# Attention and two feed-forward networks in one kernel: decoding of weight units, the softmax sum and the order of the steps rearranged

## Chip, cores and metric

One core of one Trainium2 chip runs the whole kernel as one program. The metric is the device time of one execution in microseconds. Times inside the program are counted from the start of its span; the execution's own time is a little longer than the span.

## What is computed

```python
def reference(q, k, v, w_in, w_out, w1, w2, w3, w_out2):
    # attention: B=2, H=8, S=768, D=64
    k_sum = k.reshape(B, H, 24, 32, D).max(axis=3)
    v_sum = v.reshape(B, H, 24, 32, D).mean(axis=3)
    local = where(|i - j| < 16, scale * q @ k.T, -1e9)
    block = scale * q @ k_sum.T + log(32)
    s = concatenate([local, block]); s = s - s.max()
    a = exp(s); a = a / (a.sum() + 1e-9)
    x = a @ concatenate([v, v_sum])         # as 1536 rows of 512
    # network 1, 512 -> 2048 -> 512
    h = x @ w_in;  x = (h - tanh(h)) @ w_out
    # network 2, 512 -> 1024 -> 512
    return ((x @ w1) * (x @ w2)) @ w3 @ w_out2
```

All inputs and outputs are float32. Query and key are wide enough that exp(s) has a real spread.

## The kernel before, in words

Every large product is made with operands split into a high and a low part, so that one product is three matmuls on TensorE: high by high, low by high, high by low (helper `split_mm`, lines 238 to 240). 128x512 is the usual tile.

**Weight units.** The weights come in 512 KB units of 128x512 words of 64 bits, loaded by SP in a fixed sequence (four buffers). A unit is decoded to float32 in steps: ScalarE makes `bits` (line 145); then either VectorE makes three operations (158, 160, 162), or, for units in the table `PLAN["SIGN"]`, ScalarE makes a second activation into the upper half of `dec` (149) and VectorE two operations (152, 154). A unit's high part `wh` is copied on GpSimd (191) or, for units in `PLAN["ACT"]`, on ScalarE (193); its low part `wl` is a subtraction on GpSimd (200). Units that are started while the attention runs keep `bits` in PSUM; only these can take the form with two operations.

**Stage 1, attention, 0 to about 117 us.** The work is 24 groups g, each of 4 query tiles of one pair of heads. Group g goes through S(g) (scores, TensorE), M0 to M3 (mask and maximum, VectorE), E0 to E3 (exponentials with their sum z, ScalarE), R(g) (z + 1e-9 as a sum over two columns, line 450, and its reciprocal, 451, both VectorE), PP(g) (product, GpSimd, 455), T(g) (transposes, TensorE), PB(g) (copy `pt`, ScalarE, 467), V(g) (product with the values, TensorE), XH(g) (high part, ScalarE, 488) and XL(g) (low part, VectorE, 243). V has one PSUM buffer, so V(g+1) waits for XL(g). At every third group V also makes the block means of the next pair of heads, which ScalarE copies (`vr`, 399) and SP writes into the values with three small DMAs (404). The key maxima K0 to K2 are made on VectorE and copied by GpSimd (379).

Beside this TensorE makes w34 = w3 @ w_out2 in 32 *parts* of six matmuls; these need weight units, and they are the work that fills TensorE. After four parts the sums are copied by ScalarE (337) or added by VectorE (335).

The order is written by hand as tables. Step g runs through one of three lists in `PLAN["L"]` (steps 0 and 1, steps 2 to 16, from 17); an entry such as `("T", 2)` issues T(g-2), `("S", -1)` issues S(g+1). `W0` and `W1` issue the step's parts, whose number is `PLAN["N34"][g]`; `D`, `U`, `H`, `L` and `ST` move the weight units on. Each engine runs its instructions in the order in which the lists issue them.

**Stage 2, network 1, 117 to about 375 us.** 48 steps of 24 matmuls on TensorE; the other engines make h - tanh(h) and decode the remaining units. Entry min(n, 8) of `PLAN["MIDDLE"]` is the order of step n.

**Stage 3, network 2, to the end.** The first third of the rows goes through plain products (`product_a`, `half`, `product_b`, `final`, with `w34_split` making the two parts of w34), the others through seven products instead of eight for each two by two block (`group`, `w_sums`).

Of the kernel before, what the change touches and what calls it, by code (L numbers as in the profile page):

```python
# [7 lines left out]
F32 = mybir.dt.float32  # L8
# [5 lines left out]
AF = mybir.ActivationFunctionType  # L14
ALU = mybir.AluOpType
# [6 lines left out]
P = 128  # L22
# [4 lines left out]
QT = 64  # L27
# [25 lines left out]
PLAN = {"cuts": [2, 17], "N34": [0, 0, 0, 0, 0, 2, 0, 2, 2, 0, 2, 1, 2, 1, 2, 0, 1, 2, 3, 1, 2, 1, 1, 3, 1, 2, 3],  # L53
        "MORE": (15, 18, 22), "MOREU": (20, 24, 32),
        "SIGN": (1, 3, 5, 7, 9, 11, 13, 14, 15, 17, 19, 20, 21, 22, 23, 24, 26, 27, 28, 29, 32, 35, 39, 41, 43, 45, 47, 49, 51, 53, 55, 57, 59, 61, 63, 65, 67, 69, 71, 73, 75, 77, 79), "ACT": (0, 4, 7, 8, 16, 19, 22, 25, 27, 28, 29, 31, 33, 35)}
PLAN["L"] = [
# [14 lines left out]
]  # L71
PLAN["MIDDLE"] = [
# [17 lines left out]
def fused_kernel(tc, qT, kT, vW, w_in, w_out, w1, w2, w3, wo2, out):  # L90
# [156 lines left out]
    with tc.tile_pool(name="base", bufs=1) as base, \  # L247
# [9 lines left out]
        nc.gpsimd.memset(numax, -UMAX)  # L257
        band = base.tile([P, WK], F32, name="band")
# [7 lines left out]

        mean = base.tile([P, 6 + BLK], F32, name="mean")
        nc.gpsimd.memset(mean, 0.0)

        def rows(col, a, b):  # L270

            nc.gpsimd.memset(col, 1.0 / BLK)
            for base_, step in ((-a, 1), (b - 1, -1)):
                nc.gpsimd.affine_select(out=col, in_=col, pattern=[[0, 1]], compare_op=ALU.is_ge, fill=0.0,
                                        base=base_, channel_multiplier=step)

        rest = base.tile([P, 1], F32, name="mean_rest")
        rows(mean[:, 6:7], WIN, WIN + BLK)
        rows(mean[:, 7:8], WIN + BLK, QT)
        rows(rest, CW, CW + WIN)  # L280
        nc.gpsimd.tensor_tensor(out=mean[:, 7:8], in0=mean[:, 7:8], in1=rest, op=ALU.add)
        masks = []
        for z in range(3):
            mk = base.tile([P, NC], F32, name=f"mask{z}")
            nc.gpsimd.memset(mk[:, BC], LOG_BLK)
            nc.gpsimd.tensor_copy(out=mk[:, :QT], in_=band[:, :QT])
            nc.gpsimd.tensor_copy(out=mk[:, CW:], in_=band[:, QT:])
            if z == 0:
                nc.gpsimd.memset(mk[:, :WIN], NEG)
            if z == 2:  # L290
                nc.gpsimd.memset(mk[:, NC - WIN:], NEG)
            masks.append(mk)
# [46 lines left out]
        with tc.tile_pool(name="p1", bufs=1) as p1, \  # L339
# [41 lines left out]
            sums = [p1.tile([P, TU, 2], F32, tag=f"z{i}", name=f"z_{i}") for i in range(3)]  # L381
            for i in sums:
                nc.vector.memset(i[:, :, 1], 1e-9)
# [47 lines left out]
            def mx(g, i):  # L431
                t = g % NU * TU + i
                mk = masks[0 if t == 0 else 2 if t == NQ - 1 else 1]
                if g not in nm:
                    nm[g] = p1.tile([P, TU], F32, tag="nm", bufs=3, name=f"nm_{g}")
                    pr[g] = p1.tile([P, TU, NC], F32, tag="pr", bufs=3, name=f"pr_{g}")
                    z[g] = sums[g % 3]
                nc.vector.tensor_tensor_reduce(  # L438
                    out=pr[g][:, i, :], in0=st[g][i % len(st[g])][:, i, :], in1=mk[:, :], scale=-0.125, scalar=3.0e38,
                    op0=ALU.add, op1=ALU.min, accum_out=nm[g][:, i:i + 1])  # L440

            def ex(g, i):
# [67 lines left out]
            scores(0)  # L510
            n34 = 0
# [68 lines left out]
            acts = dict(S=do_S, R=do_R, PP=do_PP, T=do_T, PB=do_PB, V=do_V, XH=do_XH, XL=do_XL)  # L580
# [395 lines left out]
        for m in range(1, NM):  # L976
# [7 lines left out]
            a = product_a(m, 0)  # L984
            wt.unit(1)
# [39 lines left out]
        for m in range(0, NM, 2):  # L1025
# [84 lines left out]
```

## Time and profile before

| what | us |
|---|---|
| runs | 574.33, 574.31, 571.29 (median 574.31) |
| the profiled execution, its own time | 572.8 |
| its span | 571.1 |
| TensorE busy | 556.0 |
| VectorE busy | 456.1 |
| ScalarE busy | 335.1 |
| GpSimd busy | 292.0 |

The trace gives for each engine the instructions with start, duration, and the idle time ahead of them with what released it. Matmuls overlap, so the time between two starts is less than a matmul's listed duration. On ScalarE and VectorE, too, the next instruction starts a little before the listed end of the one ahead.

### The profile page before, as it was taken

What the parts mean: (1) busy time and instruction counts of PE and PEld (TensorE: products, weight loads), DVE (VectorE), ACT (ScalarE), POOL (GpSimd) and SP (SyncE); (2) the same over time, 40 slices, a digit from 0 to 9 for tenths busy, and PEclk for the clock granted to TensorE, in tenths of its full rate; (3) what the DMA queues carried; (4) which work ended last, traced back from release to release, by engine and by line L of the source; (5) the groups of instructions that cost most, each with busy time, mean ns of one, the idle gap of its engine ahead of it and who ended that gap; (6) DMA issues with size and microseconds to landing.
All of it is one profiled execution on the core that took longest, in us unless ns stands there. A gap on an engine that the chain in (4) does not pass through costs nothing.

```text
span 571.1 us, 9225 instructions
## 1 busy us (share of the span) xinstructions
PE 556.0 (97%) x3224; PEld 450.0 (79%) x3224; DVE 456.1 (80%) x880; ACT 335.1 (59%) x739; POOL 292.0 (51%) x257
## 2 busy tenths in 40 slices
PE   6699999999999999999999999999999999999997
PEld 5477777778888888888888888888788877888885
DVE  4878899998899999889999769999378677868510
ACT  4799888876978876577766667845233321213110
POOL 4766775834464655535645315466536653617220
PEclk9899999999999999999999999999999999999999
DMA  8998777441232332122223003222000100000021
GB/s 329 352 312 287 279 242 231 143 146 38 74 111 76 110 100 84 37 84 87 88 82 102 1 2 110 75 73 75 0 1 1 74 1 1 1 0 1 1 92 55
DMA packets 18526, 56.56 MB, mean 99 GB/s; under 512 B 1968, under 2 KB 4656, under 8 KB 18480
## 3 DMA queue, kind: packets, MB, share of 16 engines
q1 hardware_dynamic: 18336, 55.84, 29.6%
q8 instruction: 25, 0.41, 0.3%
q14 instruction: 21, 0.17, 0.1%
q10 hardware_dynamic: 144, 0.13, 0.1%
HBM read 51.64 MB, written 3.15 MB: 96 GB/s over the span
## 4 chain that ended last, share of the span: by engine, by line
PE 81%; DVE 9%; issue 3%; ACT 3%; DMA 2%; SPq 1%; POOL 0%; DVEq 0%; ACTq 0%
PE ph L238 7%; PE ph L239 7%; PE ph L240 7%; PE x L238 7%; PE x L239 7%; PE x L240 7%; PE p_w L238 5%; PE p_w L240 5%; PE p_w L239 4%; PE o L240 4%; PE o L239 4%; PE o L238 4%; PE w34a L238 2%; DMA raw<-wo 2%; PE w34a L239 2%
## 5 line engine op out<-in xcount | busy, mean ns | idle before, releaser
L243 POOL TENSOR_TENSOR gl<-g,gh 128x512 fp32r<-128x512 f32 x48 | 65.0, 1354 | 127.1 <-ACT gh L729 69.4
L200 POOL TENSOR_TENSOR wl<-dec,wh 128x512 fp32r<-128x512 f32 x72 | 111.7, 1553 | 18.1 <-ACT wh L193 14.5
L238 PE MATMUL x<-gh,wh 128*128 128x512 f32 x192 | 74.9, 390 | 0.0
L238 PE MATMUL ph<-xh,wh 128*128 128x512 f32 x192 | 74.8, 390 | 0.0
L239 PE MATMUL x<-gl,wh 128*128 128x512 f32 x192 | 74.7, 389 | 0.0
L240 PE MATMUL ph<-xh,wl 128*128 128x512 f32 x192 | 74.7, 389 | 0.0
L239 PE MATMUL ph<-xl,wh 128*128 128x512 f32 x192 | 74.7, 389 | 0.0
L240 PE MATMUL x<-gh,wl 128*128 128x512 f32 x192 | 74.7, 389 | 0.0
L707 ACT ACTIVATE u<-ph 128x512 f32<-128x512 f32 x48 | 28.8, 600 | 52.0 <-PE ph L240 52.0
L162 DVE SCALAR_TENSOR_TENSOR dec<-raw,dec 128x512 uint32<-128x512 uint32 x48 | 48.6, 1013 | 1.5
L718 DVE TENSOR_TENSOR g<-ph,u 128x512 f32<-128x512 f32 x48 | 33.0, 687 | 17.6 <-ACT th L708 16.1
L720 DVE SCALAR_TENSOR_TENSOR g<-sq,g 128x512 f32<-128x512 f32 x48 | 45.3, 943 | 0.6 <-ACT sq L713 0.5
L243 POOL TENSOR_TENSOR s_w<-s_w,s_w 128x512 fp32r<-128x512 f32 x16 | 23.1, 1460 | 42.9 <-ACT s_w L937 23.2
L193 ACT CAST wh<-dec 128x512 fp32r<-128x512 f32 x54 | 33.7, 624 | 15.9 <-DVE dec L162 15.7
L238 PEld LDWEIGHTS x<-gh,wh 128*128 128x128 f32 x192 | 36.1, 188 | 7.9 <-DVE x2a L755 0.4
L443 ACT ACTIVATE pr<-pr,nm 128x120 f32<-128x120 f32 x96 | 37.9, 401 | 7.2 <-DVE nm L438 7.2
L240 PEld LDWEIGHTS x<-gh,wl 128*128 128x128 f32 x192 | 36.0, 188 | 7.5
L238 PEld LDWEIGHTS ph<-xh,wh 128*128 128x128 f32 x192 | 36.0, 188 | 7.5
L239 PEld LDWEIGHTS ph<-xl,wh 128*128 128x128 f32 x192 | 36.1, 188 | 7.4
L240 PEld LDWEIGHTS ph<-xh,wl 128*128 128x128 f32 x192 | 36.0, 188 | 7.5
L239 PEld LDWEIGHTS x<-gl,wh 128*128 128x128 f32 x192 | 36.0, 188 | 7.5 <-POOL gl L243 0.2
L724 DVE COPY_PREDICATED g<-mk,ph 128x512 f32<-128x512 uint32 x48 | 36.0, 749 | 3.9
(164 smaller groups left out, 1426.8 us busy)
## 6 DMA issues: line engine op xcount, KB each, us to landing
raw<-w SPq DMA_DIRECT2D x32, 512.0 KB
raw<-w_in SPq DMA_DIRECT2D x16, 512.0 KB
raw<-w_out SPq DMA_DIRECT2D x16, 512.0 KB
vg<-vW SPq DMA_DIRECT2D x8, 768.0 KB
raw<-wo SPq DMA_DIRECT2D x8, 512.0 KB
kt<-kT SPq DMA_DIRECT2D x7, 544.0 KB
qt<-qT SPq DMA_DIRECT2D x7, 384.0 KB
out<-u_out SPq DMA_DIRECT2D x6, 256.0 KB
```

What stands on the lines that cost most here:

```text
L162: lambda tu=tu, su=su, lo=lo: stt(out=tu, in0=lo, scalar=29, in1=su, op0=ALU.logical_shift_right, op1=ALU.bitwise_or)])
L193: nc.scalar.copy(out=h, in_=self.t[n])
L200: nc.gpsimd.tensor_tensor(out=l, in0=self.t[self.n_low], in1=h[:, :].bitcast(F32), op=ALU.subtract)
L238: mm(out=acc, lhsT=lh, rhs=rh, start=start, stop=False)
L239: mm(out=acc, lhsT=lh, rhs=rl, start=False, stop=False)
L240: mm(out=acc, lhsT=ll, rhs=rh, start=False, stop=stop)
L243: eng.tensor_tensor(out=out, in0=x, in1=high.bitcast(F32), op=ALU.subtract)
L443: nc.scalar.activation(out=pr[g][:, i, :], in_=pr[g][:, i, :], func=AF.Exp, scale=-1.0, bias=nm[g][:, i:i + 1], accum_out=z[g][:, i, :1])
L707: nc.scalar.activation(out=u, in_=ph, func=AF.Square)
L718: nc.vector.tensor_tensor(out=gn, in0=ph, in1=u, op=ALU.mult)
L720: nc.vector.scalar_tensor_tensor(out=gn, in0=sq, scalar=GAM, in1=gn, op0=ALU.add, op1=ALU.mult)
L724: nc.vector.copy_predicated(out=gn, mask=mask[:, :].bitcast(U32), data=ph)
```

## The change

- `PLAN["SIGN"]` grows: of the units that are started during the attention, 21 instead of 16 are decoded with two VectorE operations, and ScalarE has the second activation for the five more.
- The column of 1e-9 and the reduction over two columns are gone. A new step Z(g) adds 1e-9 to z on ScalarE with a bias tile `eps`; R(g) is the reciprocal alone.
- The lists `PLAN["L"]` have another order and the new entry Z; `PLAN["N34"]` places the parts otherwise (the first two in step 4 instead of 5; none in steps 5, 8 and 20); `MORE`, `MOREU` and the first eight entries of `MIDDLE` differ.
- The masks and `mean` are made on GpSimd behind the first key maxima, not ahead of them.
- In stage 3 `w34_split(m)` stands ahead of the unit's step and the calls of `high` and `low` ahead of it are gone; in the loop over `group` the second `next(g)` comes ahead of `w_sums`.

```diff
-PLAN = {"cuts": [2, 17], "N34": [0, 0, 0, 0, 0, 2, 0, 2, 2, 0, 2, 1, 2, 1, 2, 0, 1, 2, 3, 1, 2, 1, 1, 3, 1, 2, 3],
+PLAN = {"cuts": [2, 17], "N34": [0, 0, 0, 0, 2, 0, 1, 2, 0, 1, 2, 1, 1, 2, 1, 1, 1, 2, 3, 1, 0, 3, 1, 3, 2, 1, 3],
...
+        eps = base.tile([P, 1], F32, name="eps")
+        nc.gpsimd.memset(eps, 1e-9)
...
-            sums = [p1.tile([P, TU, 2], F32, tag=f"z{i}", name=f"z_{i}") for i in range(3)]
-            for i in sums:
-                nc.vector.memset(i[:, :, 1], 1e-9)
...
-                    z[g] = sums[g % 3]
+                    z[g] = p1.tile([P, TU], F32, tag="z", bufs=3, name=f"z_{g}")
...
+            def softmax_z(g):
+                nc.scalar.activation(out=z[g], in_=z[g], func=AF.Identity, bias=eps[:])
 
             def softmax_r(g):
                 rs[g] = r = p1.tile([P, TU], F32, tag="r", bufs=2, name=f"r_{g}")
-                nc.vector.tensor_reduce(out=r, in_=z[g], axis=AX.X, op=ALU.add)
-                nc.vector.reciprocal(out=r, in_=r)
+                nc.vector.reciprocal(out=r, in_=z[g])
...
             a = product_a(m, 0)
+            w34_split(m)
             wt.unit(1)
...
-            if m > 2:
-                wt.high()
-                wt.low()
-            w34_split(m)
             final(*prev)
...
             next(g)
+            next(g)
             sums = w_sums("w2", m)
             next(sums)
-            next(g)
             lhs = next(sums)
```

The order on GpSimd at the start of the program, before (`kt` is the key tile that the copy completes, `pr` the probabilities):

```order
L281 TENSOR_TENSOR mean<-mean,mean_rest 128x1
L285 MEMSET mask_102 128x24
L286 COPY mask_102<-band 128x64
L287 COPY mask_102<-band 128x32
...
L291 MEMSET mask_111 128x16
L379 COPY kt_156<-kb_176 128x12x24
L455 TENSOR_TENSOR pr_189<-pr_189,r_248 128x480
```

And now, behind the making of `band`:

```order
L267 AFFINE_SELECT band<-band 64x96
L355 COPY kt_125<-kb_145 128x12x24
L489 MEMSET mask_157 128x24
L490 COPY mask_157<-band 128x64
L491 COPY mask_157<-band 128x32
...
L511 TENSOR_TENSOR mean<-mean,mean_rest 128x1
L430 TENSOR_TENSOR pr_185<-pr_185,r_243 128x480
```

The copy into `kt` moved ahead of the three masks and of `mean`.

On TensorE, from V(0) on, before (`av` is V's bank, `t` T's, `s` S's, `w34a` the sums of w34):

```order
L477 MATMUL av_366<-pt_299,vg_164 64x64 x8
L394 MATMUL av_366<-vg_201,mean 32x128 x12
L462 MATMUL t_405<-ident,pr_245 120x128 x4
L428 MATMUL s_3_425<-kt_166,qt_168 64x120 x2
L428 MATMUL s_4_426<-kt_166,qt_168 64x120 x2
...
L477 MATMUL av_445<-pt_344,vg_164 64x64 x8
L238 MATMUL w34a_0_460<-wh_294,wh_321 128x512
L239 MATMUL w34a_0_460<-wl_295,wh_321 128x512
L240 MATMUL w34a_0_460<-wh_294,wl_322 128x512
```

And now:

```order
L452 MATMUL av_364<-pt_309,vg_133 64x64 x8
L367 MATMUL av_364<-vg_198,mean 32x128 x12
L239 MATMUL w34a_0_398<-wh_301,wh_316 128x512
L240 MATMUL w34a_0_398<-wl_302,wh_316 128x512
L241 MATMUL w34a_0_398<-wh_301,wl_317 128x512
...
L437 MATMUL t_417<-ident,pr_246 120x128 x4
L401 MATMUL s_3_422<-kt_135,qt_137 64x120 x2
...
L452 MATMUL av_455<-pt_356,vg_133 64x64 x8
```

Part 0 moved ahead of T(2), S(5) and V(1); part 1 stands between S(5) and V(1).

On ScalarE at the second weight unit, before:

```order
L145 ACTIVATE bits_215<-raw_162 128x512
L443 ACTIVATE pr_207,z_143<-pr_207,nm_206 128x120 x4
L399 COPY vr_258<-pvs 96x128
L145 ACTIVATE bits_267<-raw_170 128x512
L149 ACTIVATE dec_266<-raw_170 128x512
L443 ACTIVATE pr_245,z_144<-pr_245,nm_244 128x120 x2
L193 CAST wh_294<-dec_214 128x512
```

And now:

```order
L146 ACTIVATE bits_209<-raw_131 128x512
L416 ACTIVATE pr_185,z_186<-pr_185,nm_184 128x120 x2
L422 ACTIVATE z_186<-z_186,eps 128x4
L416 ACTIVATE pr_203,z_204<-pr_203,nm_202 128x120 x2
L146 ACTIVATE bits_257<-raw_139 128x512
L150 ACTIVATE dec_256<-raw_139 128x512
L372 COPY vr_265<-pvs 96x128
L416 ACTIVATE pr_203,z_204<-pr_203,nm_202 128x120
```

The second unit's two activations moved ahead of two of group 1's exponentials and of the copy `vr`, and the new activation of z stands between the exponentials.

## Rows read from the trace of the kernel before

**Rows 1.** The page, its first part: busy time of each engine.

```profile
PE 556.0 (97%) x3224; PEld 450.0 (79%) x3224; DVE 456.1 (80%) x880; ACT 335.1 (59%) x739; POOL 292.0 (51%) x257
```

**Rows 2.** Stretches: length, busy time by engine (PE to POOL), PEclk, DMA, GB/s.

```profile
0.00:26.20 26.20, 15.96 (x197) 12.67 (x197) 15.64 (x79) 15.83 (x55) 15.19 (x47) 0.98 0.94 339
24.97:75.54 50.57, 50.01 (x632) 37.84 (x634) 42.49 (x180) 44.79 (x154) 34.75 (x39) 0.97 0.88 302
117.00:375.00 258.00, 257.96 (x1150) 213.24 (x1151) 233.37 (x330) 186.41 (x333) 124.17 (x84) 1.00 0.25 78
23.00:25.00 2.00, 0.87 (x19) 0.47 (x17) 1.86 (x9) 2.00 (x10) 1.92 (x3) 1.00 1.03 404
25.00:27.00 2.00, 1.86 (x18) 1.65 (x19) 2.00 (x12) 1.99 (x8) 2.00 (x3) 0.53 1.03 411
```

**Rows 3.** TensorE in order of time: start, duration, instruction, [idle before <-releaser].

```profile
19.31 0.69 PE L477 MATMUL av<-pt,vg 120*64 120x64 f32 x16 [0.64 <-DMA vg<-vr]
19.92 1.07 PE L394 MATMUL av<-vg,mean 128*32 128x128 f32 x24
22.65 0.65 PE L462 MATMUL t<-ident,pr 128*120 128x128 f32 x4 [1.65 <-POOL pr L455]
...
26.20 0.80 PE L238 MATMUL w34a<-wh,wh 128*128 128x512 f32 x1
...
28.76 0.60 PE L462 MATMUL t<-ident,pr 128*120 128x128 f32 x4
...
31.15 0.39 PE L240 MATMUL w34a<-wh,wl 128*128 128x512 f32 x1
```

**Rows 4.** GpSimd in order of time: the copy into the key tile.

```profile
6.40 0.42 POOL L379 COPY kt<-kb 128x288 f32<-128x288 f32 x1
```

**Rows 5.** VectorE in order of time: the key maxima of that copy.

```profile
5.12 0.20 DVE L377 TENSOR_REDUCE kb<-hb 128x24 f32<-128x48 f32 x1
```

**Rows 6.** ScalarE in order of time, 12 to 25 us.

```profile
12.86 0.25 ACT L399 COPY vr<-pvs 96x128 f32<-96x128 f32 x1
13.46 0.64 ACT L145 ACTIVATE bits<-raw 128x512 f32<-128x512 f32 x1 [0.35 <-DMA raw<-w]
...
15.67 0.62 ACT L193 CAST wh<-dec 128x512 fp32r<-128x512 f32 x1
...
19.08 0.64 ACT L145 ACTIVATE bits<-raw 128x512 f32<-128x512 f32 x1 [1.93 <-DMA raw<-wo]
...
22.21 0.79 ACT L149 ACTIVATE dec<-raw 128x512 f16<-128x512 f32 x1
22.84 0.25 ACT L399 COPY vr<-av 96x128 f32<-96x128 f32 x1
22.98 0.40 ACT L443 ACTIVATE pr<-pr,nm 128x120 f32<-128x120 f32 x1
...
23.37 0.37 ACT L488 CAST xh<-av 128x256 fp32r<-128x256 f32 x1
...
24.39 0.58 ACT L467 COPY pt<-t 120x512 f32<-120x512 f32 x1
```

**Rows 7.** ScalarE's groups, 24.9 to 75.6 us: busy, mean ns | idle before, releaser.

```profile
L467 ACT COPY pt<-t 120x512 f32<-120x512 f32 x13 | 7.6, 587 | 2.9 <-PE t L462 2.9
...
L488 ACT CAST xh<-av 128x256 fp32r<-128x256 f32 x12 | 4.4, 371 | 0.8 <-PE av L477 0.8
...
L399 ACT COPY vr<-av 96x128 f32<-96x128 f32 x4 | 1.0, 262 | 2.1 <-PE av L394 2.0
```

**Rows 8.** VectorE's groups, 0 to 117 us, columns as in rows 7.

```profile
L152 DVE TENSOR_SCALAR dec<-raw 128x512 uint16<-128x512 uint16 x16 | 12.1, 756 | 0.0
L154 DVE SCALAR_TENSOR_TENSOR dec<-bits,dec 128x512 uint32<-128x512 uint32 x16 | 11.0, 685 | 1.7 <-ACT dec L149 1.3
...
L158 DVE TENSOR_SCALAR bits<-bits 128x512 uint32<-128x512 uint32 x8 | 5.6, 698 | 3.0 <-ACT bits L145 2.7
...
L450 DVE TENSOR_REDUCE r<-z 128x4 f32<-128x8 f32 x24 | 3.6, 151 | 1.1 <-ACT pr L443 1.1
```

More of the change, by code (lines that the diff above doesn't have):

```diff
@@ L51 @@
 FLUSH = 4
-PLAN = {"cuts": [2, 17], "N34": [0, 0, 0, 0, 0, 2, 0, 2, 2, 0, 2, 1, 2, 1, 2, 0, 1, 2, 3, 1, 2, 1, 1, 3, 1, 2, 3],
-        "MORE": (15, 18, 22), "MOREU": (20, 24, 32),
-        "SIGN": (1, 3, 5, 7, 9, 11, 13, 14, 15, 17, 19, 20, 21, 22, 23, 24, 26, 27, 28, 29, 32, 35, 39, 41, 43, 45, 47, 49, 51, 53, 55, 57, 59, 61, 63, 65, 67, 69, 71, 73, 75, 77, 79), "ACT": (0, 4, 7, 8, 16, 19, 22, 25, 27, 28, 29, 31, 33, 35)}
+PLAN = {"cuts": [2, 17], "N34": [0, 0, 0, 0, 2, 0, 1, 2, 0, 1, 2, 1, 1, 2, 1, 1, 1, 2, 3, 1, 0, 3, 1, 3, 2, 1, 3],
+        "MORE": (15, 18, 22, 27), "MOREU": (20, 28),
+        "SIGN": (1, 3, 4, 5, 6, 7, 9, 10, 11, 12, 13, 14, 15, 17, 18, 19, 20, 21, 22, 23, 24, 25, 26, 27, 28, 29, 30, 31, 33, 34, 35, 36, 37, 38, 39, 41, 43, 45, 47, 49, 51, 53, 55, 57, 59, 61, 63, 65, 67, 69, 71, 73, 75, 77, 79), "ACT": (0, 1, 4, 7, 16, 19, 22, 25, 27, 28, 29, 31, 32, 33, 35, 37, 38)}
 PLAN["L"] = [
[14 rows of a table removed]
[15 rows of a table added]
 ]
 PLAN["MIDDLE"] = [
[8 rows of a table removed]
[8 rows of a table added]
     ["HID", "ST", "H", "EV", "C", "U", "UT", "G", "SM", "MM", "L", "RS", "BK"],
@@ L265, in fused_kernel @@
                                     fill=NEG, base=2 * WIN - 1, channel_multiplier=1)
[L267 to L292, printed above, removed]
         w34 = [base.tile([P, DM], F32, tag=f"w34_{i}", name=f"w34_{i}") for i in range(NM)]
@@ L443, in ex @@
                 nc.scalar.activation(out=pr[g][:, i, :], in_=pr[g][:, i, :], func=AF.Exp, scale=-1.0,
-                                     bias=nm[g][:, i:i + 1], accum_out=z[g][:, i, :1])
+                                     bias=nm[g][:, i:i + 1], accum_out=z[g][:, i:i + 1])
             rs = {}
+            def softmax_z(g):
+                nc.scalar.activation(out=z[g], in_=z[g], func=AF.Identity, bias=eps[:])
             def softmax_r(g):
                 rs[g] = r = p1.tile([P, TU], F32, tag="r", bufs=2, name=f"r_{g}")
-                nc.vector.tensor_reduce(out=r, in_=z[g], axis=AX.X, op=ALU.add)
-                nc.vector.reciprocal(out=r, in_=r)
+                nc.vector.reciprocal(out=r, in_=z[g])
             def softmax_p(g):
@@ L510, in fused_kernel, with rows @@
             scores(0)
+            masks = []
+            for i in range(3):
+                mk = base.tile([P, NC], F32, name=f"mask{i}")
+                nc.gpsimd.memset(mk[:, BC], LOG_BLK)
+                nc.gpsimd.tensor_copy(out=mk[:, :QT], in_=band[:, :QT])
+                nc.gpsimd.tensor_copy(out=mk[:, CW:], in_=band[:, QT:])
+                if i == 0:
+                    nc.gpsimd.memset(mk[:, :WIN], NEG)
+                if i == 2:
+                    nc.gpsimd.memset(mk[:, NC - WIN:], NEG)
+                masks.append(mk)
+            mean = base.tile([P, 6 + BLK], F32, name="mean")
+            nc.gpsimd.memset(mean, 0.0)
+            def rows(col, a, b):
+                nc.gpsimd.memset(col, 1.0 / BLK)
+                for base_, step in ((-a, 1), (b - 1, -1)):
+                    nc.gpsimd.affine_select(out=col, in_=col, pattern=[[0, 1]], compare_op=ALU.is_ge, fill=0.0,
+                                            base=base_, channel_multiplier=step)
+            rest = base.tile([P, 1], F32, name="mean_rest")
+            rows(mean[:, 6:7], WIN, WIN + BLK)
+            rows(mean[:, 7:8], WIN + BLK, QT)
+            rows(rest, CW, CW + WIN)
+            nc.gpsimd.tensor_tensor(out=mean[:, 7:8], in0=mean[:, 7:8], in1=rest, op=ALU.add)
             n34 = 0
@@ L553, in order, with do_Z, do_R @@
                 return (0, 2, 1, 3)[i] if g >= ALL else i
-            def do_R(g):
+            def do_Z(g):
                 for i in range(4):
                     need("E%d" % i, g)
+                softmax_z(g)
+            def do_R(g):
+                need("Z", g)
                 softmax_r(g)
@@ L579, in do_XL @@
                 x_low(g)
-            acts = dict(S=do_S, R=do_R, PP=do_PP, T=do_T, PB=do_PB, V=do_V, XH=do_XH, XL=do_XL)
+            acts = dict(S=do_S, Z=do_Z, R=do_R, PP=do_PP, T=do_T, PB=do_PB, V=do_V, XH=do_XH, XL=do_XL)
             for i in range(4):
```

45 rows, old and new, of the table PLAN are left out of this document.

## The prediction

> **What bounds the kernel now.** I read the page first. TensorE is busy 556.0 of 571.1 us [rows 1], and the order of its 2303 rows holds the same work before and after; so the time can only move by TensorE's idle time (15.1 us) and by stretches at the lower of its two clock levels. The table of stretches says where the idle time lies [rows 2]: 15.96 of the first 26.20 us are busy, so 10.2 us of it are there and 4.9 us are left for everything behind, the closing output transfer included. In the middle stage 257.96 of 258 us are busy. In 25 to 27 us the granted clock is 0.53, so the engine ran mostly at its 1.2 GHz level there; in the 2 us ahead of it TensorE was busy 0.87 us. The other stretches of these rows stand at or near the 2.4 GHz level.
>
> The first 26 us are a start-up whose pieces wait for each other [rows 3]: values of group 0 at 19.31 us (waited for a transfer), transposes of group 2 at 22.65 (waited 1.65 us for GpSimd's product), the first w34 part at 26.20. From there TensorE is full, and the other engines have slack that differs: in 24.97 to 75.54 us, which is from the end of PB(2) to the end of PB(14), ScalarE is busy 44.79 us and VectorE 42.49 of 50.57 [rows 2]. ScalarE's 5.8 us of idle time there are waits for TensorE [rows 7]. So now TensorE sets the pace and ScalarE follows closest behind.
>
> **The change part by part.** *Masks later.* GpSimd makes `mean` and the masks first and copies the key maxima, which the first scores wait for, at 6.40 us; VectorE had them ready at 5.12 + 0.20 = 5.32 us [rows 4, 5]. The first scores and exponentials come 1.0 us earlier. This does not last. On ScalarE the second weight unit's `bits` now stands ahead of two of group 1's exponentials and of the copy `vr`; its raw data landed at about 13.46 us [rows 6], and the loads ahead of it are the same and in the same order. So ScalarE waits for that transfer some 2 us instead of working past it. `vr`, which was copied at 12.86 us, its three DMAs on SP and all loads behind them on SP start about 2 us later. They landed at 19.31 us right behind the third raw unit at 19.08 [rows 3, 6], because the queues were full, and I let them land at 19.4 again. Gain of this part: 0, and at worst 2 us if the three small transfers take their full time behind the later issue.
>
> *First w34 parts earlier.* Before, order on TensorE after the values of group 0 is T(2), S(5), V(1), part 0, T(3), S(6), part 1, and the last of these ends at 31.15 + 0.24 = 31.4 us [rows 3]. Now it is part 0, T(2), S(5), part 1, V(1), T(3), S(6): the same seven pieces. Values of group 0 with the block means from 19.4 to 21.1 us (1.68 as before); part 0 at the low clock 2.56 us (26.20 to 28.76 before) until 23.7, its third matmul's low part being ready at about 21.5 (ScalarE's `wh` behind the third unit's `bits`, then GpSimd); T(2) and S(5) about 0.65 each, until 25.0; V(1) 0.69; then T(3), S(6) and a part together 2.64 (28.76 to 31.4 before), until 28.3. That is **3.1 us earlier** than 31.4, idle time filled with work that has to be done anyway.
>
> *Five more units joined by two VectorE operations.* The order has 21 instead of 16 units in that form. VectorE loses 5 x 3 operations, all taken like the first of them at 0.698 = 10.5 us, and gains 5 x (0.756 + 0.685) = 7.2: 3.3 us less [rows 8]. ScalarE gets 5 more `dec` activations, which take 0.63 each until the next starts [rows 6]: 3.2 us more.
>
> *z + 1e-9 on ScalarE.* VectorE loses 24 reductions of 0.151 = 3.6 us [rows 8]. ScalarE gets 24 activations of 128x4 with a bias tile. No row shows one. The nearest below is the `vr` copy, 128 columns without a bias tile, 0.14 us until the next starts; the nearest above is an exponential of 120 columns with one, 0.39 [rows 6]. I take 0.20, since the four columns lie near the short end, and the bias tile adds something: 4.8 us in all, 3.4 to 9.4 at the ends. In the main lists the exponential it depends on lies well ahead on ScalarE, so it does not stall there; the reciprocal, GpSimd's product and XL on VectorE, which frees the bank of the next values, now come behind it and so behind two exponentials of the next group. The Trainium skill, page "ScalarE: Activation LUTs", section "What ACT_TABLE_LOAD costs", gives about 280 ns for an activation with a pointer bias, of which some 93 ns overlap the next one: an estimate of 0.19 each and 4.6 us in all, so the sum would stay what it is; no run here shows it yet.
>
> *What ScalarE's load makes of the gain.* From the end of PB(2) to the end of PB(14) the order of ScalarE gains 4 `dec`, 12 z activations and loses one `wh` copy (0.62 us): 44.79 + 2.52 + 2.40 - 0.62 = 49.1 us. PB(2) itself ends later: from the third `bits` at 19.08 us to the end of PB(2) (24.39 + 0.58 = 24.97) ScalarE now has one `wh`, one exponential and two z activations more, 0.62 + 0.39 + 0.40 = 1.4, so 26.4 us. A ScalarE that never waits then ends PB(14) at 26.4 + 49.1 = 75.5 us, where it was 75.54 [rows 2, 6]. Up to that step both versions have done 15 parts. So the 3.1 us are **given back**: TensorE runs ahead, waits at V for XL and at T for the product, and meets step 16 where it was. Never waiting is too good: ScalarE waited 5.8 us for TensorE; with TensorE ahead, most of that goes; I keep 0.4 us, with 0 and 5.8 as ends.
>
> *Behind step 16* two or three parts stand in a step, TensorE is the longer one again, and the parts done are equal within two at each step; only step 20 now has no part. Steps without one ran before too (4, 6, 9, 15) with TensorE full: 0. VectorE's 3.3 + 3.6 = 6.9 us less are no gain, since TensorE hardly waits for it.
>
> *Middle and end.* Only entries 0 to 7 of the middle's lists differ; the ninth, which every later step uses, is the same. With 257.96 of 258 us busy there is nothing to win, and cover is what VectorE has left (233.37 of 258). `w34_split` earlier and the second `next(g)` ahead of the sums move single operations of ScalarE, GpSimd and VectorE by a product or two; TensorE's 4.9 us of idle time behind 26.2 us bound all of it. 0; if the cover fails, one operation of about 0.7 us.
>
> **The rivals.** *A, ScalarE keeps up.* If the z activation is at 0.14 or less and the exponentials wait less because VectorE is freer, TensorE keeps its lead: 572.8 - 3.1 = 569.7 us. For it: ScalarE had 5.8 us of idle time. Against: 4.9 us of new work in the same stretch, and PB(2) later. *B, ScalarE sets the pace and still waits.* TensorE's steps have no, one or two parts, ScalarE's have their own long and short ones, and if neither can run ahead by a step, ScalarE's old waits stay: 2.9 us for transposes, 2.1 and 0.8 for values [rows 7]. PB(14) then ends at 75.5 + 5.8, and the time is 572.8 + 5.8 = 578.6 us. It decides as soon as ScalarE needs more than the 50.6 us of that stretch; with 49.1 it is 1.5 us short of it. The Trainium skill, page "ScalarE: Activation LUTs", section "Rules for kernel authors", puts adds on VectorE and not on ScalarE, and by that rule it goes this way; the trace so far agrees in that ScalarE is the busier of the two in this stretch, 44.79 against 42.49. *C, the change has no hold on the time*: the start is set by transfers (V(0) at 19.4 us either way) and all else is covered; then 572.8 us, which lies inside my forecast.
>
> **How the numbers follow.** The profiled execution took 572.8 us, span 571.1 and 1.7 around it. 572.8 - 3.1 (start filled) + 3.1 (given back at ScalarE's pace) + 0.4 (waits that stay) = 573.2 us. The runs of before were 574.33, 574.31 and 571.29, median 574.31; the profiled one lies in the middle of their spread, so I keep the sum as it is and read "faster" and "slower" against the median: about 0.5% of it, 2.9 us, is what a measurement of this kernel can tell from no change, so under 571.4 and over 577.2. The forecast, with C, has 0.59 (571.4 to 576), A 0.27, B 0.14. Faster 0.27, same 0.59, slower 0.14. The range takes most of A and the near part of B: 569.8 to 577.0.
>
> **What would show it.** First scores at 5.9 us instead of 6.88, values of group 0 still at 19 to 20. T(3) and S(6) done by about 28 us. ScalarE with under 2 us of idle time from PB(2) to PB(14), and TensorE with new waits of about 1 us each for XL or the product between 28 and 47 us; if these are missing, A is right; if ScalarE shows over 3 us of waits for TensorE there, B. PB(14) should end near 75.5 us. The middle should stay at 258 of 258. What would make all of this wrong: a z activation that holds ScalarE longer than an exponential does, transfers of K or V that land late because SP issues them in another order, or a wait at the first steps of the middle.

## The result, and the profile after

The changed kernel takes **581.23 us** (median of 6 runs, 580.44 to 581.49) where the kernel before takes 573.38 (median of 6): ratio 1.015, 95% interval 1.0133 to 1.0167. It is slower by 7.9 us, which lies outside the range of the prediction. The profiled execution has a span of 578.7 us, 7.6 more than before.

The busy line of the page answers to [rows 1]:

```profile
PE 564.6 (98%) x3224; PEld 451.0 (78%) x3224; DVE 444.8 (77%) x848; ACT 342.1 (59%) x768; POOL 291.2 (50%) x258
```

VectorE lost 11.3 us and ScalarE gained 7.0, as the change meant. But TensorE, with the same 3224 matmuls, is busy for 8.6 us longer, while its idle time fell from 15.1 to 14.1 us. To see where, I split both executions at the first matmul on `ph`, which ends the attention. The columns are those of [rows 2]. Before:

```profile
0.00:117.66 117.66, 106.36 (x1257) 81.13 (x1257) 95.74 (x374) 94.93 (x312) 80.03 (x113) 0.99 0.79 271
117.66:571.10 453.44, 449.64 (x1972) 368.91 (x1968) 360.40 (x507) 240.21 (x427) 211.92 (x145) 1.00 0.17 54
```

After:

```profile
0.00:118.06 118.06, 107.67 (x1256) 81.39 (x1257) 87.18 (x342) 102.27 (x341) 77.49 (x113) 0.99 0.77 267
118.06:578.70 460.64, 456.95 (x1972) 369.58 (x1968) 357.67 (x507) 239.84 (x428) 213.73 (x145) 1.00 0.17 54
...
117.00:375.00 258.00, 257.85 (x1129) 209.12 (x1128) 230.56 (x325) 183.41 (x330) 122.11 (x82) 1.00 0.25 76
```

The attention, where the change acts, ends 0.4 us later in these two executions. The other 7.2 us are in the **second part**, from that matmul to the end: the same 1972 matmuls at the full clock, and TensorE 456.95 us busy in place of 449.64. In 117 to 375 us it is busy throughout in both kernels, but 1129 matmuls fit in it where 1150 did [rows 2]. A busy share of 100% hides this; the count beside it shows it.

The timeline shows it matmul by matmul (start, duration, operation). Before:

```profile
119.15 0.39 PE L238 MATMUL ph<-xh,wh 128*128 128x512 f32 x1
...
122.78 0.39 PE L239 MATMUL ph<-xl,wh 128*128 128x512 f32 x1
```

After:

```profile
118.86 0.39 PE L239 MATMUL ph<-xh,wh 128*128 128x512 f32 x1
...
122.61 0.40 PE L240 MATMUL ph<-xl,wh 128*128 128x512 f32 x1
```

Sixteen steps lie between the two rows each time: 3.63 us before (227 ns a step), 3.75 after (234 ns). The duration in the row hardly changes, because matmuls overlap; the start-to-start time is what counts. Its mean over all neighbours with 512 columns and the same output, with no idle time between them, is, in ns, before and after: `ph` 227.0 and 233.7, `w` 227.1 and 234.1, `p_w` 229.8 and 233.6, `o` 231.7 and 232.4, `x` 227.3 and 228.4, and `w34a`, steps of over 300 ns left out, 231.2 and 231.4. With 576, 192, 336, 288 and 576 of the first five this makes 3.9 + 1.3 + 1.3 + 0.2 + 0.6 = 7.3 us. So the matmuls that read the attention's result (`xh`, `xl`) slowed by 4 to 7 ns, those of `o` and `x` by about 1, and those of `w34a` did not.

No line of the diff touches them. What it did move is memory: three masks and `mean` are now made, and given their place, behind `xh` and `xl` instead of ahead of them, and `eps` takes 32 bytes. In the places that the compiler gave the tiles, in bytes of a partition, the distance from `xh` to the weights `wh` was 109216 - 35488 = 73728, a multiple of 256; now it is 109248 - 33888 = 75360, which is 96 more than one. The 1632 bytes between the two are the three masks (480 each), `mean` (160) and its helper tile `mean_rest` (32), which now lie between `xl` and the weights. From the weights to `gh`, the operand of `x`, it stays 81920, a multiple of 256; why `x` still slows by 1 ns, no run says.

### The profile page after: what moved, and what is told of

Same layout as the page of the kernel before. It is cut to its first block, busy times and chain, and to the rows that moved or that the text cites. A ratio compares the mean times of both kernels' runs of the same rounds, so it can differ in the third digit from the quotient of the medians.

```text
span 578.7 us, 9190 instructions
## 1 busy us (share of the span) xinstructions
PE 564.6 (98%) x3224; PEld 451.0 (78%) x3224; DVE 444.8 (77%) x848; ACT 342.1 (59%) x768; POOL 291.2 (50%) x258
## 4 chain that ended last, share of the span: by engine, by line
PE 86%; ACT 6%; DVE 3%; DMA 1%; POOL 1%; issue 1%; SPq 1%; ACTq 0%; POOLq 0%; DVEq 0%
PE ph L241 8%; PE ph L240 8%; PE ph L239 8%; PE x L239 7%; PE x L240 7%; PE x L241 7%; PE p_w L239 5%; PE p_w L241 5%; PE p_w L240 5%; PE o L241 4%; PE o L240 4%; PE o L239 4%; PE w L241 3%; PE w L239 3%; PE w L240 3%; ACT pr L416 2%
## 5 line engine op out<-in xcount | busy, mean ns | idle before, releaser
L241 PE MATMUL ph<-xh,wl 128*128 128x512 f32 x192 | 76.3, 397 | 0.0
L240 PE MATMUL ph<-xl,wh 128*128 128x512 f32 x192 | 76.1, 396 | 0.0
L722 DVE TENSOR_TENSOR g<-ph,u 128x512 f32<-128x512 f32 x48 | 33.0, 687 | 19.4 <-ACT th L712 18.8
L724 DVE SCALAR_TENSOR_TENSOR g<-sq,g 128x512 f32<-128x512 f32 x48 | 46.8, 976 | 0.2 <-ACT sq L717 0.2
```

What stands on the lines that cost most here:

```text
L240: mm(out=acc, lhsT=lh, rhs=rl, start=False, stop=False)
L241: mm(out=acc, lhsT=ll, rhs=rh, start=False, stop=stop)
L722: nc.vector.tensor_tensor(out=gn, in0=ph, in1=u, op=ALU.mult)
L724: nc.vector.scalar_tensor_tensor(out=gn, in0=sq, scalar=GAM, in1=gn, op0=ALU.add, op1=ALU.mult)
```

## The experiments

Two theories. **Place**: a matmul's rate depends on where its two operands lie in SBUF. **Traffic**: the other engines do more or other work beside the matmuls and slow them. This table has all runs of the whole kernel; "first part" ends with the first matmul on `ph`, as above, and both parts are from the profiled execution. Each ratio is against runs of the kernel before on the same chip. Read a first part with care: after, e1 and e2 run the same order and work there, and took 118.06, 118.87 and 120.69 us, so a difference of under 3 us between two first parts is not shown by them alone. The second part is steadier: 453.2 to 454.8 us in all 13 runs at a multiple of 256.

| run | distance from x to weights, over a multiple of 256 | first part, us | second part, us | median, us | ratio (95%) |
|---|---|---|---|---|---|
| before | 0 | 117.66 | 453.44 | 573.38 | |
| after | 96 | 118.06 | 460.64 | 581.23 | 1.015 (1.0133 to 1.0167) |
| e1, after, places of before | 0 | 118.87 | 454.03 | 575.54 | 1.0062 (1.0041 to 1.0084) |
| e2, after, 416 bytes unused | 0 | 120.69 | 453.61 | 575.99 | 1.0069 (1.0046 to 1.0093) |
| e3, before, masks moved | 96 | 116.76 | 460.44 | 579.2 | 1.0128 (1.0105 to 1.0152) |
| e4, before, 32 bytes unused | 32 | 118.42 | 460.38 | 580.51, one run | |
| e5, before, 64 bytes unused | 64 | 117.21 | 459.09 | 578.07, one run | |
| e6, before, all 32 bytes up | 0 | 117.41 | 453.19 | 572.56 | 0.9995 (0.9979 to 1.001) |
| e8, e1 and 15 matmuls | 0 | 120.96 | 453.94 | 576.63 | 1.0065 (1.0049 to 1.0081) |
| e9, e1 and 6 matmuls | 0 | 118.21 | 453.99 | 574.25 | 1.0018 (0.9998 to 1.0039) |
| e10, e1, z on VectorE | 0 | 119.49 | 453.91 | 575.02 | 1.0035 (1.0019 to 1.0051) |
| e11, e1, old order | 0 | 121.66 | 453.84 | 577.83 | 1.0066 (1.0042 to 1.0089) |
| f1, before, all 96 bytes up | 0 | 117.76 | 453.24 | 573.02 | 1.0012 (0.9996 to 1.0028) |
| f2, f1 and 3 matmuls | 0 | 117.91 | 453.19 | 572.39 | 1.0001 (0.9985 to 1.0017) |
| f3, e9, all 96 bytes up | 0 | 119.41 | 453.79 | 574.76 | 1.0043 (1.0027 to 1.006) |
| f4, after, 160 bytes unused, 6 matmuls | 0 | 118.25 | 453.55 | 574.83 | 1.005 (1.003 to 1.007) |
| f5, f4, old units, z on VectorE | 0 | 123.93 | 454.77 | 581.95 | 1.0168 (1.0142 to 1.0195) |

### Is it the place?

e1 is the changed kernel with every tile where it was before:

```diff
-        nsb = base.tile([P, 1], F32, name="nsb")
-        eps = base.tile([P, 1], F32, name="eps")
+        pair = base.tile([P, 2], F32, name="nsb")
+        nsb, eps = pair[:, 0:1], pair[:, 1:2]
...
+        mean = base.tile([P, 6 + BLK], F32, name="mean")
+        rest = base.tile([P, 1], F32, name="mean_rest")
+        mks = [base.tile([P, NC], F32, name=f"mask{i}") for i in range(3)]
         w34 = [...]
```

> The changed kernel, with mean and masks given their places in SBUF ahead of w34, xh and xl as in the kernel before (only the places; they are still written late), and eps beside nsb in one tile. So xh, xl and the weight parts lie at the same bytes as before (35488, 60064, 109216). Theory 'place': TensorE's matmuls became slower because xh, xl and the parts lie elsewhere; then the ph matmuls start every 227 ns again instead of 234, and the time is 573.2 us, that of the prediction (571.5 to 576). Theory 'traffic': they became slower because the other engines' work is mixed differently; then 234 ns and 581 us stay.

e2 is the changed kernel with 416 unused bytes behind `xl`, e4 the kernel before with 32:

```diff
         xl = [base.tile([P, KC, TB], F32R, name=f"xl_{k}") for k in range(NTB)]
+        pad = base.tile([P, 104], F32, name="pad")
+        nc.gpsimd.memset(pad[:, :1], 0.0)
```

> The changed kernel with an unused tile of 416 bytes between xl's block and the raw units, which puts the parts a whole multiple of 2048 bytes from xh and xl again (both at 1120 within 2048), at other absolute places than before. Theory 'place, distance counts': 227 ns for ph, 573 us. Theory 'place, absolute bytes count': somewhere else, 581 or in between. Theory 'traffic': 234 ns, 581 us.

e3 is the kernel before with only the lines that allocate `w34`, `xh` and `xl` ahead of `mean` and the masks:

```diff
+        w34 = [...]
+        xh = [...]
+        xl = [...]
         mean = base.tile([P, 6 + BLK], F32, name="mean")
```

> The kernel before, with nothing changed but that mean and masks get their places in SBUF behind xl instead of ahead of w34: xh then lies at 1088 within 2048, the parts stay at 672. Same instructions, same order. Theory 'place': ph matmuls start every 234 ns instead of 227 and the time is 8 us longer, 581 us. Theory 'traffic': no change, 573 us.

> The kernel before, with an unused tile of 32 bytes behind xl: the parts and the second stage's tiles move by 32 bytes against xh and xl (which stay). Theory 'place, distance counts in whole 2048': ph at 234 ns, about 580 us. 'Place, only coarse distance counts' (hundreds of bytes): ph stays at 227 ns, 573 us. 'Traffic': 573 us.

In before, after and e1 to e4 the second part falls into two groups, 453.4 to 454.0 us and 460.4 to 460.6, and the distance alone says which. e3 against the two rows of before above:

```profile
0.00:116.76 116.76, 106.60 (x1257) 81.11 (x1257) 95.70 (x374) 95.04 (x312) 80.12 (x113) 0.99 0.79 273
116.76:577.20 460.44, 456.87 (x1972) 369.63 (x1968) 361.40 (x507) 239.75 (x427) 210.80 (x145) 1.00 0.17 54
```

The work of all engines is that of before, and still TensorE is busy for 7.2 us more in the second part (456.87 against 449.64). Traffic is out; place is shown, in both directions.

### Which distances?

```diff
         xl = [base.tile([P, KC, TB], F32R, name=f"xl_{k}") for k in range(NTB)]
+        pad = base.tile([P, 16], F32, name="pad")
+        nc.gpsimd.memset(pad[:, :1], 0.0)
```

> The kernel before, with an unused tile of 64 bytes per partition between the low parts of x and the pools behind it (32 bytes made it 580.5 us). All tiles that the matmuls read keep their offset within 64 bytes (32), but the weights now lie 64 bytes off a multiple of 512 from x. If what counts is that both operands of a matmul have the same offset within 64 bytes: 572 to 573 us, and 227 ns from one matmul with 512 columns to the next on ph and p_w. If the distance has to be a multiple of 512 or 2048 bytes: 579 to 581 us and 233 to 234 ns, as with 32 bytes.

e6, and f1 further down, have the unused tile (32 and 96 bytes) ahead of `ident` instead, so that all tiles move together.

> The kernel before, with an unused tile of 32 bytes ahead of all others, so that x, the weights, gh and w34 all start at a multiple of 64 bytes (before: all 32 bytes behind one); the distances between them stay. If only the two operands' offsets against each other count: within 1 us of before, 227 ns. If a start at a multiple of 64 bytes counts by itself and helps: below 570 us, and under 227 ns. If x at a multiple of 64 is what hurt in the changed kernel's neighbour (before with the masks moved): 579 us.

e7 and e12 measure the matmul by itself. One tile `big`; a section accumulates in one bank, with its moving operand `mo` and its stationary operand `so` bytes into the tile:

```diff
+            for i in range(N):
+                a, b = mo // 4 + 512 * (i % 8), so // 4 + 512 * (i % 3)
+                nc.tensor.matmul(out=acc, lhsT=big[:, b:b + P], rhs=big[:, a:a + 512],
+                                 start=i == 0, stop=i == N - 1)
```

(e7: 48 matmuls, the stationary operand in steps of 128 columns through 24 places.)

> Not the computation: only matmuls with 512 columns in one tile, 48 for each of 24 pairs of offsets within 64 bytes and beyond (moving operand, stationary operand), first with all other engines silent, then the last 6 pairs with VectorE and ScalarE copying in SBUF beside them. If the place acts in TensorE alone: pairs with the same offset take 227 ns or less from one matmul to the next and pairs that differ by 32 bytes some 6 ns more, in the silent part too. If it acts only through the other engines' accesses: all silent pairs alike, a difference only in the last 6. If the distance counts beyond 64 bytes: the pairs at 64, 128 and 256 bytes differ from the pair at 0.

> Not the computation: matmuls with 512 columns, 24 for each of 32 distances between stationary and moving operand (steps of 64 bytes over 2048), then 7 larger distances and 8 pairs of places at equal or known distances; all other engines silent. If what counts is the distance modulo 256 bytes: 227 ns at each fourth step, 230 to 234 at the others. If it has to be a multiple of 512 or 2048: 227 ns at each eighth step, or at one alone. If an offset is better than all that the kernels use, it shows as less than 226 ns.

TensorE in e12, in order of time: start, duration, section. From `daa` (distance 0) each section adds 64 bytes, so `dae` is at 256 and `dai` at 512:

```profile
44.07 5.60 PE L36 MATMUL daa<-big 128*128 128x512 f32 x24
49.51 5.76 PE L36 MATMUL dab<-big 128*128 128x512 f32 x24
55.11 5.74 PE L36 MATMUL dac<-big 128*128 128x512 f32 x24
60.68 5.67 PE L36 MATMUL dad<-big 128*128 128x512 f32 x24
66.19 5.61 PE L36 MATMUL dae<-big 128*128 128x512 f32 x24
71.64 5.76 PE L36 MATMUL daf<-big 128*128 128x512 f32 x24
77.24 5.74 PE L36 MATMUL dag<-big 128*128 128x512 f32 x24
82.82 5.67 PE L36 MATMUL dah<-big 128*128 128x512 f32 x24
88.33 5.61 PE L36 MATMUL dai<-big 128*128 128x512 f32 x24
```

The starts lie 5.44, 5.60, 5.57, 5.51, and again 5.45, 5.60, 5.58, 5.51 us apart; over 24 that is 226.7, 233.3, 232.1, 229.6 ns, and the same four repeat through all 32 sections. **The step is 256 bytes**; nothing beats a multiple of it, and larger distances, up to 56 tiles of 2 KB further off, give the same 227 ns. The changed kernel's own distance, 96 bytes beyond, stands in e7 (`qh`; its 48 matmuls end where `qi` starts):

```profile
88.40 11.40 PE L35 MATMUL qh<-big 128*128 128x512 f32 x48
99.64 11.32 PE L35 MATMUL qi<-big 128*128 128x512 f32 x48
```

That is 11.24 us, or 234.2 ns each, what `ph` takes in the changed kernel, with no other engine at work. In e7 the pairs at 32 and 32 bytes (`ql`, `lc`) and at 32 and 64 (`qm`, `ld`) stand once in the silent part and once beside VectorE and ScalarE at work:

```profile
132.89 11.08 PE L35 MATMUL ql<-big 128*128 128x512 f32 x48
143.81 11.35 PE L35 MATMUL qm<-big 128*128 128x512 f32 x48
155.00 11.36 PE L35 MATMUL qn<-big 128*128 128x512 f32 x48
...
232.71 11.06 PE L35 MATMUL lc<-big 128*128 128x512 f32 x48
243.60 11.35 PE L35 MATMUL ld<-big 128*128 128x512 f32 x48
254.79 11.06 PE L35 MATMUL le<-big 128*128 128x512 f32 x48
```

From start to start 48 matmuls take 10.92 and 10.89 us at an equal place, 11.19 and 11.19 at 32 bytes between them: with VectorE busy for 27.4 and ScalarE for 31.4 of the 33 us from `lc` on the times are the same.

So my theory of equal offsets within 64 bytes fell: e5 keeps them and takes 459.09 us in its second part, and a distance of 64 costs 233.3 ns.

### What is left of the change

Without the place, 0.6% is left in e1. Its TensorE waits from 14.6 to 18.2 us for `pt` of group 0 and then gets a lower clock. e8 and e9 put unused matmuls there (`busy(n)` multiplies `ident` by itself n times; 15 in e8):

```diff
             def do_T(g):
                 need("PP", g)
+                if g == 1:
+                    busy(6)
                 transposes(g)
```

> The changed kernel with all tiles at the addresses of before (575.5 us, 0.6% over before), and 15 unused matmuls ahead of the transposes of group 1, in the 3.6 us in which TensorE waits at 14.6 to 18.2 us and after which its granted clock was 0.50 to 0.77 until 25 us. If that low clock is what is left of the 0.6%: the granted clock stays at 1.00 there and the time falls by 2 to 3.5 us, to 572 to 573.5. If ScalarE's larger load sets the pace from 25 to 75 us: the start comes earlier, but the probabilities of group 14 still end near 75 us and the time stays at 574.5 to 576.

> As the changed kernel at the addresses of before with 15 unused matmuls, but 6, since 15 took 8.1 us where 3.6 were free and put the transposes of group 1 off from 18.2 to 22.6 us. If the low clock after the idle 3.6 us is what is left of the 0.6%: PB(3) starts near 29.3 us (30.51 without them) and the time is 573 to 574. If the start-up's order itself costs it: PB(3) near 30.5 and 575 to 576.

Stretches of e1, columns as above (TensorE's busy time first, its granted clock third from the end):

```profile
15.00:17.00 2.00, 0.00 (x0) 0.00 (x0) 0.65 (x2) 2.00 (x10) 0.39 (x1) 1.00 0.85 307
17.00:19.00 2.00, 0.79 (x4) 0.70 (x4) 0.91 (x9) 1.70 (x6) 1.83 (x2) 0.52 0.68 102
19.00:21.00 2.00, 2.00 (x32) 1.48 (x32) 1.87 (x4) 2.00 (x9) 1.39 (x2) 0.50 0.91 337
21.00:23.00 2.00, 2.00 (x32) 1.50 (x28) 1.94 (x11) 1.71 (x5) 1.92 (x3) 0.50 0.99 310
```

And of e9:

```profile
15.00:17.00 2.00, 1.77 (x9) 1.18 (x8) 0.62 (x2) 2.00 (x11) 0.36 (x1) 1.00 0.91 337
17.00:19.00 2.00, 1.46 (x16) 0.93 (x19) 1.09 (x10) 1.93 (x6) 1.85 (x2) 1.00 0.65 84
19.00:21.00 2.00, 1.28 (x38) 1.01 (x33) 1.91 (x4) 2.00 (x11) 1.57 (x2) 1.00 0.91 293
21.00:23.00 2.00, 2.00 (x29) 1.62 (x24) 1.74 (x11) 1.49 (x4) 1.92 (x3) 1.00 0.94 305
```

In e1 TensorE runs at the 1.2 GHz level from 17 to 23 us, behind a stretch of 2 us with no matmul; in e9 it stays at 2.4 GHz. That holds beyond the two traces: the granted clock, averaged over each execution, is 0.991 to 0.994 in all five runs of e1 and 0.996 to 1.000 in all ten of e9, and the ratio falls from 1.0062 to 1.0018. The 31 runs of the kernel before beside f1 to f4 show what the low clock is worth: eight with a mean of 0.987 to 0.991 took 573.7 to 575.3 us (median 574.3), the 23 with 0.993 to 0.997 a median of 572.1, some 2 us less. Much of the spread between executions of one kernel goes with it. In e8 the clock stayed up too, but 15 matmuls took 8.1 us where 3.6 were free, the first part came 2.75 us later than in e9, and the time with it: in these two runs a delay at 20 us was still there at 118. The filler is not sure, though: in f3 and f4 it stood at the same place and the clock was at 0.50 in 21 to 23 and in 19 to 21 us of the profiled execution.

e10 takes z off ScalarE, e11 takes the new order back (the lists `PLAN["L"]` and `PLAN["N34"]` of before, with `("Z", 1)` ahead of each `("R", 1)`):

```diff
-                nc.scalar.activation(out=z[g], in_=z[g], func=AF.Identity, bias=eps[:])
+                nc.vector.tensor_scalar(out=z[g], in0=z[g], scalar1=1e-9, scalar2=None, op0=ALU.add)
```

> The changed kernel at the addresses of before, with z + 1e-9 as an addition on VectorE in place of ScalarE's activation (0.29 us, 24 of them). If ScalarE's load sets the pace from 25 to 75 us: ScalarE has some 3 us less to do in PB(3) to PB(14), PB(14) comes up to 3 us earlier and the time is 573 to 574. If ScalarE only fills what it has (its waits come back) or VectorE takes its place: 575 to 576, and PB(14) stays at 75 us.

> The changed kernel at the addresses of before, with the order inside the attention's steps and w34's split of before; the joined units, z on ScalarE and the later masks stay. If the new order costs the 0.6% (the idle 3.6 us and the low clock behind them): 572.5 to 574. If the joined units and z on ScalarE cost it: 575 to 577, and ScalarE waits for nothing between 25 and 75 us.

31 to 75 us, e1 and then e10:

```profile
31.00:75.00 44.00, 42.21 (x554) 31.75 (x552) 33.41 (x138) 43.84 (x153) 30.89 (x34) 1.00 0.84 298
```

```profile
31.00:75.00 44.00, 42.13 (x546) 31.64 (x540) 37.63 (x155) 42.38 (x140) 30.63 (x35) 1.00 0.83 299
```

In e1 ScalarE is busy for 43.84 of 44 us. e10 relieves it by 1.5 us, and in this execution TensorE gets no further: 42.13 us busy against 42.21. But e10 also puts 4.2 us on VectorE, and its ratio (1.0035) and that of e1 (1.0062) have intervals that overlap, so it does not settle whether ScalarE sets the pace. e11 did not go as expected: with the new work on ScalarE and the old order ScalarE was busy for only 40.65 of the 44 us, most of its idle time (2.9 us) being waits for TensorE again, and the first part was 2.8 us longer than in e1 and 4.0 longer than before. So the new order gives back most of what the new work and the later masks cost under the old one. The times of the runs say the same (577.2 to 578.2 us against 574.6 to 576.9 in e1), but the two ratios, 1.0066 and 1.0062, do not separate them: 2.8 us is the figure of two executions.

### Both edits, and is there a better kernel?

f4 is the changed kernel with 160 unused bytes behind `xl` and the 6 matmuls. f1 to f3 look for more, f5 takes ScalarE's load back in f4 (`SIGN`, `ACT`, `MORE` and `MOREU` of before, z as in e10). f2 has `if g == 2: busy(3)`.

> The changed kernel with two edits: an unused tile of 160 bytes behind the low parts of x, which makes the distance from x to the weights a multiple of 256 bytes and of nothing larger, and the 6 unused matmuls ahead of the transposes of group 1. If 256 bytes is the step and the low clock the rest: 573.5 to 575 us, 227 ns on ph and p_w near 229. If the distance must be a multiple of 512 or 2048: 579 to 580.5.

> The kernel before with an unused tile of 96 bytes ahead of all others, so that x, the weights, gh and w34 start at multiples of 256 bytes (160 behind one before); their distances stay. If only the distance counts: within 0.1% of before. If the place of the moving operand itself counts too, as the pairs in the run with matmuls alone had it (226.7 against 228.5 ns): up to 1 ns for each of some 2300 matmuls, 0.5 to 2 us faster.

> The same, with 3 unused matmuls ahead of the transposes of group 2, in the 1.65 us in which TensorE waited for GpSimd's product before its clock fell to 0.53 and 0.62 in 25 to 29 us. If the low clock there costs what its length says (2.6 us at half the rate): 1 to 1.4 us faster than without them. If the stage then waits for ScalarE: no difference, and the first matmul of the middle stage starts at the same time.

> The changed kernel with the distances of before, 6 unused matmuls in its idle 3.6 us (574.25 us so far) and all tiles at multiples of 256 bytes. If the place of the moving operand counts: 572 to 573.5. If not: 574 to 574.5, and the kernel before stays ahead of it or level with it.

> The changed kernel with the 160 bytes and the 6 unused matmuls (574.83 us), and with ScalarE's load as before: the units that were joined by three VectorE operations are so again, their copies are where they were, and z + 1e-9 is added on VectorE; the new order and the later masks stay. If ScalarE's load holds the attention back: ScalarE has idle time again in 31 to 75 us, PB(23) comes before 113.4 us (114.1 with the load) and the time is 571.5 to 573. If VectorE or the order sets the pace then: 574 to 576, PB(23) at 114 or later.

f4 has none of before's addresses, and its second part is that of before:

```profile
0.00:118.25 118.25, 108.99 (x1268) 82.12 (x1268) 87.17 (x342) 102.43 (x341) 77.46 (x114) 0.99 0.77 267
118.25:571.80 453.55, 449.12 (x1972) 368.89 (x1968) 356.70 (x507) 240.34 (x428) 213.85 (x145) 1.00 0.17 55
```

160 bytes take 6.4 of the 7.9 us back (581.23 to 574.83, the 6 matmuls included). Tiles at multiples of 256 bytes gave nothing beyond an equal distance (f1, f3). In f2 the clock had fallen ahead of the unused matmuls, at 17 to 23 us, so it does not say what that low clock costs. f5 went the other way: without the joined units and with z on VectorE, VectorE is late for the new order (TensorE waited 3.3 us for `xl` between 30 and 130 us, 1.4 in f4), and the first part grows by 5.7 us. No run is faster than the kernel before by more than its interval. The 0.5% that f4 keeps over it were not traced to one operation; for e9, at 0.2%, the interval reaches 1.

## Why the prediction was wrong

**The step that failed** is in the first sentence of its first part: the order holds the same work, "so the time can only move by TensorE's idle time (15.1 us) and by stretches at the lower of its two clock levels". That takes the time of a matmul as fixed. It went from 227 to 234 ns on `ph` and `w`, which with `p_w`, `o` and `x` makes some 7.3 us, the 7.2 of the second part, and *Middle and end: 0* fell with it. The sign of trouble that the prediction named, "the middle should stay at 258 of 258", could not have caught this: it stayed at 257.85. The one thing in the diff that mattered stood under *Masks later*: it was costed as GpSimd's time, and the allocation that moved along was not costed.

What the prediction says of the attention came out nearly as worked out on ScalarE and less well on TensorE. That it had 0.4 us in all and the first part of the profiled execution is 0.40 us longer is in part luck: e1 and e2, with the same order, ended theirs 1.2 and 3.0 us later than before, and with the place mended they take 0.6 and 0.7% more than before, not 0.1. TensorE after, in order of time, answers to [rows 3]:

```profile
5.84 5.07 PE L401 MATMUL s<-kt,qt 64*64 64x120 f32 x48 [1.06 <-POOL kt L355]
...
18.45 0.88 PE L437 MATMUL t<-ident,pr 128*120 128x128 f32 x4 [3.72 <-ACT pt L442]
...
20.26 1.12 PE L452 MATMUL av<-pt,vg 120*64 120x64 f32 x16
...
27.47 0.65 PE L437 MATMUL t<-ident,pr 128*120 128x128 f32 x4
28.70 0.74 PE L401 MATMUL s<-kt,qt 64*64 64x120 f32 x16 [0.57 <-POOL kt L355]
```

ScalarE after, answering to [rows 6]:

```profile
13.40 0.64 ACT L146 ACTIVATE bits<-raw 128x512 f32<-128x512 f32 x1 [1.27 <-DMA raw<-w]
...
16.27 0.29 ACT L422 ACTIVATE z<-z,eps 128x4 f32<-128x4 f32 x1
16.46 0.39 ACT L416 ACTIVATE pr<-pr,nm 128x120 f32<-128x120 f32 x1
...
17.73 0.57 ACT L442 COPY pt<-t 120x512 f32<-120x512 f32 x1
```

```profile
25.61 0.57 ACT L442 COPY pt<-t 120x512 f32<-120x512 f32 x1
...
74.54 0.56 ACT L442 COPY pt<-t 120x512 f32<-120x512 f32 x1
```

- *Masks later*: first scores at 5.84 us (5.9 foretold), and the gain was lost again. The place of the loss was another: not a transfer but `pt` of group 0, which ScalarE makes at 17.73 us (16.19 before): it waited for the raw data of the second unit until 13.40 and had that unit's two activations, the copy `vr`, six exponentials, a z and a `wh` copy to do from there. V(0) starts at 20.26, not at 19.4.
- *First w34 parts earlier*: T(3) and S(6) are done at 29.4 us, 2.0 earlier than the 31.4 of before and not 3.1. V(0) starts 0.9 us later than the 19.4 taken; it and the block means last 2.4 us instead of 1.7, at the low clock (granted 0.50 in 19 to 21 us, behind the wait of 3.7 us); `kt` is 0.57 us late. Part 0, which the prediction had put at the low clock, ran at the high one and gave 1.1 us back.
- *Five more units*: 21 units in that form, as counted.
- *z on ScalarE*: a z activation lasts 0.29 us, but the next instruction starts 0.19 later (16.27 to 16.46), so the 0.20 taken was right. The figures of the Trainium skill, page "ScalarE: Activation LUTs", section "What ACT_TABLE_LOAD costs", had given an estimate of 0.19 for it; the trace agrees, with these 0.19.
- *What ScalarE's load makes of the gain*: foretold was a ScalarE that never waits and PB(14) ending at 75.5 us. It was busy for 50.42 of the 50.57 us of 24.97 to 75.54. PB(2) ended at 26.18 (26.4 foretold) and PB(14) at 75.10, so the work between them took 48.9 us, where 49.1 had been worked out. That the order gains about as much as the load costs, e11 bears out as far as one execution can: 2.8 and 4.0 us. That ScalarE *sets* the pace is not shown: e10 does not settle it, and in f5, without the load, VectorE was late instead.
- *Waits that stay*, 0.4 us: from 28 to 76 us TensorE waited 1.8 us (0.7 for `xl`, 0.6 for `kt`, 0.5 for `wl`) where it had waited 0.2; no wait for the product was among them.
- The rivals: A did not happen; C holds for the first part alone. B's time, 578.6 us, is close to what was measured and for another reason: ScalarE's old waits did not come back with the new order (they did in e11, with the old one). The rule on adds by which the prediction tied it to the Trainium skill, page "ScalarE: Activation LUTs", section "Rules for kernel authors", made no clear difference here: with the addition on VectorE (e10) the median was 0.5 us shorter than in e1, and the two intervals overlap.

Without the place the sum, 573.2 us, would have been 2.3 to 2.8 us short (e1 575.54, e2 575.99), and 1.1 to 1.6 with the 6 unused matmuls, which the change does not have (e9 574.25, f4 574.83). Of the 2.3 us of e1, 1.3 go with the low clock (e1 to e9); the rest stays open.

## What to carry to other kernels

When a diff moves, adds or resizes a tile in a pool, look at where all tiles behind it land, and count the matmuls in a fixed full stretch before and after: a busy share of 100% says nothing of their rate. Here the two operands of each matmul belong at a distance that is a multiple of 256 bytes in a partition; an unused tile of the right size brought the second part back to that of before (e2, f4). Where the clock falls in the start-up changes between executions of one order (before at 25 to 29 us; f2 from 17 to 25 us, beginning ahead of its edit), so judge a filler by the granted clocks and times of many runs, not by one trace.

## What the runs showed of the hardware

- A matmul with 512 columns, both operands float32r in SBUF, takes 226.7 ns from start to start where the operands start a multiple of 256 bytes apart, and 233.3, 232.1 and 229.6 ns where they start 64, 128 and 192 bytes beyond one (e12, other engines silent). This is TensorE's own: beside busy VectorE and ScalarE the same pairs took the same time (e7). The Trainium skill, page "SBUF — State Buffer", section "Who interferes with whom", gives TensorE two independent read ports, one for the moving operand and one for the weights, and lets it wait for no other engine; the second fits e7, but the 6.6 ns show that the two operands are not indifferent to each other.
- At an equal distance the places themselves changed the time in the runs with matmuls alone: 226.7 to 227.1 ns with both operands a multiple of 256 bytes into the tile `big`, 228.3 to 228.8 with both 64, 128 or 672 bytes in (e12), 233.3 with both 16 bytes in (e7). `big` itself starts, in the compiled program, at byte 16512 of a partition, 128 beyond a multiple of 256, so f1 and f3, which put the kernel's operands at multiples of 256, did not put them where e12 was best. In the whole kernel the place made no difference: `ph` took 227.0, 226.9 and 227.0 ns a step with both operands 160, 192 and 0 bytes beyond a multiple of 256 (before, e6, f1).
- Why 256 bytes, no run here says.
